# Single-bank accumulators for two Strassen-Winograd products, and three moved pieces around them

## The chip, the cores and the metric

One core of a Trainium2 chip runs the whole program. The metric is the device time of one execution in microseconds. TensorE (PE) multiplies and writes into PSUM, which has eight banks of 512 float32 values in each of 128 partitions. VectorE (DVE) and ScalarE (ACT) read PSUM and write SBUF, GpSimd (POOL) works in SBUF, and SyncE (SP) issues most of the DMAs; POOL issues the stores of the result, which scatter rows.

## The reference, cut to what matters

```python
scores = scale * np.matmul(q, k.transpose(0, 1, 3, 2)) - np.log(S)
x = np.matmul(1.0 / (1.0 + np.exp(-scores)), v)          # 4 x 12 heads, 448 x 64
x = x.transpose(0, 2, 1, 3).reshape(1792, 768)
out[mask] = gate_w[mask, None] * (np.maximum(x[mask] @ w1[e], 0.0) @ w2[e])   # 8 experts, top 1
g = out @ w_gate                                          # 768 -> 1536
h = g * (1.0 / (1.0 + np.exp(-g))) * (out @ w_val)
return h @ w_out                                          # 1536 -> 768
```

The change touches only the last two lines: the gate and value products with the SwiGLU behind them, and the output product.

## The kernel before, in words

Attention and the experts take the first half of the span. From about 500 us on the kernel computes the two last products, each by the seven products of the Strassen-Winograd scheme, n = 1 to 7. Every operand is split into a high part and a residual, and each product is three matmuls (high-high, high-low, low-high).

**First product** (`strassen`, L950): 24 block rows r, each with n = 1..7. Rows 0 to 11 are done on the first half of the tokens, rows 12 to 23 on the second. Even r are gate weights, odd r value weights, so a pair (r, r+1) makes one block of h. One product (r, n) is nine matmuls. The order of the products is the list `steps`. In the pairs (0, 1), (10, 11) and (12, 13) it alternates the two rows for each n, in the order 1, 6, 5, 7, 2, 4, 3 (for the pair (0, 1) both rows of n = 1 and of n = 2 come first); in all other pairs one row is done before the other, in the order 1, 6, 5, 7, 2, 3, 4.

**Accumulators.** n = 1 and then 2 accumulate in a bank called a (tile `pa`), n = 5 and 3 in c (`pc`), n = 7 and 4 in d (`pd`); n = 6 has b (`pb`), from the pool `ps_t` of two banks that the transposes use as well. The tiles a, c and d are made for a pair of rows: one tile of two banks, one bank for each row. `ps_b` holds one such pair tile for a, `ps_a` two for c and d. Waits are kept by tile, so an instruction on one row's bank can have to wait for an instruction on the other row's.

**What empties them** (`evac`): ACT copies n = 1 (L991; the first at L1422) and n = 5 (L997) to SBUF; VectorE adds that copy to n = 6 (L994, u) and n = 7 (L1000, c); after n = 3 and 4 it adds u (L1008); a sigmoid on ACT (L973) and products on VectorE or POOL (L974, L978) finish a tile, and h goes to DRAM (L980, L982).

**Weights** are loaded (`w<-wgd`, L791), some summed by POOL (`sr`, L805), cast by ACT (`wgh`, L828), and VectorE takes the residual (`wgl`, L831), which is issued five products ahead of the matmuls; the sums are kept in DRAM (`wsd`, L835). SP issues loads and stores in the order in which the program emits them. The inputs are transposed by PE (L889) and split by ACT and VectorE (L923, L924). Between the products of this stage blocks of w_out are still prepared for the second product: `room` is loaded (L151), split and combined (L158 to L174, L1310) and stored.

**Second product** (`product2`, L1543): pairs of token blocks q = 0 to 6 with n = 1..7; one product is 18 matmuls. q = 0 and 1 alternate for each n, the others do not. The operand h is cast by ACT (`hhi`, L1500) and its residual taken by VectorE (`hlo`, L1504). The output weights of n = 5, 7, 2, 4, 3 (`wo`, three pieces each) are loaded when the first product ends and split during the first twelve steps (`split_wo`, casts on ACT at L80, residuals on VectorE at L81). The results are evacuated at L1580 to L1599 and stored by POOL: whole rows with `perm_c` (L1561), and for the last block half rows with `permh` (L1566).

Of the kernel before, what the change touches and what calls it, by code (L numbers as in the profile page):

```python
# [9 lines left out]
F32 = mybir.dt.float32  # L10
# [12 lines left out]
def sigmoid_attention_moe_swiglu_kernel(  # L23
# [18 lines left out]
    P = 128  # L42
# [9 lines left out]
    HW = DM // 2  # L52
# [12 lines left out]
    PS = bass.MemoryType.PSUM  # L65
# [113 lines left out]
    with ExitStack() as actx:  # L179
# [7 lines left out]
        ps_t = actx.enter_context(tc.tile_pool(name="ps_t", bufs=4, space=PS))  # L187
# [6 lines left out]
        n = B * G  # L194
# [553 lines left out]
    ectx = ExitStack()  # L748
    early = ectx.enter_context(tc.tile_pool(name="early", bufs=2, side="right", reuse_waits="tile"))
    ps_t = ctx.enter_context(tc.tile_pool(name="pst", bufs=2, space=PS, reuse_waits="tile"))  # L750
    ps_a = ctx.enter_context(tc.tile_pool(name="psa", bufs=2, space=PS, reuse_waits="tile"))
    ps_b = ctx.enter_context(tc.tile_pool(name="psb", bufs=1, space=PS, reuse_waits="tile"))
    mctx = ExitStack()
    wh = mctx.enter_context(tc.tile_pool(name="wh", bufs=LA + 1, reuse_waits="tile"))
    xp = mctx.enter_context(tc.tile_pool(name="xp", bufs=2, reuse_waits="tile"))
# [4 lines left out]
    TH = NT // 4  # L760
# [6 lines left out]
    R1 = 2 * NP  # L767
# [103 lines left out]
    tr = {}  # L871
# [54 lines left out]
    def make_xc(pool, n):  # L926
        xc[n] = tuple(pool.tile([P, K3, TH], F32R, tag=f"x{i}{n}", name=f"x{i}{n}", bufs=1)
                      for i in range(2))

    banks = {}  # L930
    sb = {}

    def strassen(r, n):
        if (r // 2, "a") not in banks:
            banks[r // 2, "a"] = ps_b.tile([P, 2, 512], F32, tag="b", name="pa")
        if n == 5 and (r // 2, "c") not in banks:
            banks[r // 2, "c"] = ps_a.tile([P, 2, 512], F32, tag="a", name="pc")
        if n == 7 and (r // 2, "d") not in banks:
            banks[r // 2, "d"] = ps_a.tile([P, 2, 512], F32, tag="a", name="pd")
        if n == 6:  # L940
            banks[r, "b"] = ps_t.tile([P, 512], F32, tag="tr", name="pb")
            ps = banks[r, "b"][:, :TH]
        else:
            ps = bank(r, {1: "a", 2: "a", 5: "c", 3: "c", 7: "d", 4: "d"}[n])
        hi, lo = wst.pop((r, n))
        xh, xl = xc[n]
        for j in range(K3):
            a = slice(j * P, (j + 1) * P)
            for st, mv, m in ((hi, xh, 0), (hi, xl, 1), (lo, xh, 2)):
                nc.tensor.matmul(ps, st[:, a], mv[:, j],  # L950
                                 start=(j == 0 and m == 0 and n not in (2, 3, 4)),
                                 stop=(j == K3 - 1 and m == 2), skip_group_check=True)

    def bank(r, nm):
        return banks[r // 2, nm][:, r % 2, :TH]

    def et(tag, bufs):
        return evp.tile([P, TH], F32, tag=tag, name=tag, bufs=bufs)
# [26 lines left out]
    def evac(r, n):  # L985
# [19 lines left out]
        else:  # L1005
# [1 line left out]
            t = et("c", 3) if steps[min(k // 14 * 14 + 13, len(steps) - 1)][1] == n else ps  # L1007
            V.tensor_add(t, ps, sb[r, "u"])  # L1008
            finish_tile(k + 1, r, *{3: (1, 2), 4: (2, 1)}[n], t, V)

    turn = [2]

    def wide(name):
        turn[0] += 1
        pool, tag = ((ps_a, "a"), (ps_a, "a"), (ps_b, "b"))[(turn[0] - 1) % 3]
        return pool.tile([P, 2, 512], F32, tag=tag, name=name)

    ev = {}
    nv = {}
# [65 lines left out]
    last = {}  # L1085
# [18 lines left out]
    def plain(kind, s, j):  # L1104
        return kind == 1 and s == L and j >= J32
# [187 lines left out]
    JO = 3  # L1293
    room = {}

    def load_o(j, x):
        load_r64(room["ro", x], ("o", j + x * KD))
# [33 lines left out]
    for j in range(JO):  # L1331
        c = 6 * j
# [52 lines left out]
    with tc.manual_schedule():  # L1385
# [24 lines left out]
        for idx, key in enumerate(seq):  # L1410
            if idx + LA < len(seq) and not plain(*seq[idx + LA]):
                split_w(*seq[idx + LA])
            for f in at.get(key, ()):
                f()
            if key == (1, 2, 0):
                nsl = nc.values_load(nslots[0:1, 0:1], min_val=0, max_val=NS,
                                     skip_runtime_bounds_check_because=why)
            product(*key)
        strassen(0, 1)
        yout(L)  # L1420
        ystore_rows(L)
# [4 lines left out]
        def between():  # L1426
            nonlocal evp, post
            with tc.If(nsl > NS0):
                extra()
            mctx.close()  # L1430
            rctx.close()
            post = ctx.enter_context(tc.tile_pool(name="post", bufs=1, reuse_waits="tile"))
            xcb = gctx.enter_context(tc.tile_pool(name="xcb", bufs=1, reuse_waits="tile"))
            for n in (6, 5, 7, 4, 3):
                make_xc(xcb, n)
            evp = gctx.enter_context(tc.tile_pool(name="evp", bufs=1, reuse_waits="tile"))
# [82 lines left out]
        banks2 = {}  # L1519
        sb2 = {}  # L1520

        def bank2(q, nm):
            return banks2[q // 2, nm][:, q % 2, :HW]

        def product2(q, n):
            if (q // 2, "a") not in banks2:
                banks2[q // 2, "a"] = ps_b.tile([P, 2, 512], F32, tag="b", name="oa")
            for m, nm in ((5, "c"), (7, "d")):
                if n == m and (q // 2, nm) not in banks2:
                    banks2[q // 2, nm] = ps_a.tile([P, 2, 512], F32, tag="a", name="o" + nm)  # L1530
            if n == 6:
                banks2[q, "b"] = ps_t.tile([P, 512], F32, tag="tr", name="ob")
                ps = banks2[q, "b"][:, :HW]
            else:
                ps = bank2(q, {1: "a", 2: "a", 5: "c", 3: "c", 7: "d", 4: "d"}[n])
            wh_, wl_ = wo[n]
            for h in range(2):
                hi, lo = hst.pop((q, n, h))
                for j in range(K3):
                    a = slice(j * P, (j + 1) * P)  # L1540
                    ws_ = slice((h * K3 + j) * HW, (h * K3 + j + 1) * HW)
                    for st, mv, m in ((hi, wh_, 0), (hi, wl_, 1), (lo, wh_, 2)):
                        nc.tensor.matmul(  # L1543
                            ps, st[:, a], mv[:, ws_],
                            start=(h == 0 and j == 0 and m == 0 and n not in (2, 3, 4)),
                            stop=(h == 1 and j == K3 - 1 and m == 2), skip_group_check=True)
# [24 lines left out]
        def later2(i, f):  # L1571
            due2.setdefault(max(i, state2["now"]), []).append(f)

        def evac2(q, n):
            V = nc.vector
            k = place2[q, n] + 1
            last = q == NQ - 1
            if n == 1:
                t = sb2[q, "p1"] = small("p")
                nc.scalar.copy(t, bank2(q, "a"))  # L1580
            elif n == 6:
                t = sb2[q, "u"] = small("u")
                V.tensor_add(t, banks2.pop((q, "b"))[:, :HW], sb2.pop((q, "p1")))
            elif n == 5:
                t = sb2[q, "p5"] = small("p")
                nc.scalar.copy(t, bank2(q, "c"))
            elif n == 7:
                t = out_tile(q, 2)[:, 1]
                V.tensor_add(t, bank2(q, "d"), sb2.pop((q, "p5")))
                V.tensor_add(t, t, sb2[q, "u"])  # L1590
                if last:
                    later2(k, lambda: store(q, 2, 1))
            elif n == 2:
                nc.scalar.copy(out_tile(q, 1)[:, 0], bank2(q, "a"))
                if last:
                    later2(k, lambda: store(q, 1, 0))
            else:
                i, m = {3: (1, 1), 4: (2, 0)}[n]
                V.tensor_add(sb2[q, i][:, m], bank2(q, {3: "c", 4: "d"}[n]), sb2[q, "u"])  # L1599
                later2(k, lambda: store(q, i, m if last else None))  # L1600

        todo = {}

# [34 lines left out]

        for j in range(JO, KD):
            if j <= JO + 1:  # L1640
                key = ((1, 6), (R1 + 1, 5))[j - JO]
                at_step(*key, lambda j=j: next_room(j))
            b0 = ((2, 1), (R1 + 2, 6), (R1 + 2, 6))[j - JO]
            d = 20 * (j == KD - 1)
            for x in range(2):
                for g in range(4):
                    at_step(*b0, lambda j=j, x=x, g=g: convert_o(j, x, g), d + 8 * x + 2 * g)
            for h in range(2):
                at_step(*b0, lambda h=h: combine_o(h), d + 15 + 2 * h)
                at_step(*b0, lambda j=j, h=h: store_o(j, h), d + 17 + h)  # L1650
            if j == JO + 1:
                at_step(*b0, lambda j=j: load_o(j + 1, 0), d + 6)
                at_step(*b0, lambda j=j: load_o(j + 1, 1), d + 14)
# [89 lines left out]
        for i, (q, n) in enumerate(steps2):  # L1743
            product2(q, n)
            later2(i + 1, lambda q=q, n=n: evac2(q, n))
            state2["now"] = i
            while i in due2:
                for f in due2.pop(i):
                    f()
            prep2_to(2 * i + 6)  # L1750
            if i < 10:
                for k in ((3 * i) // 2, (3 * i) // 2 + 1)[:1 + i % 2]:
                    split_wo(*rest[k])
        for i in range(len(steps2), len(steps2) + 3):
            state2["now"] = i
# [63 lines left out]
```

## Time and profile before

| | us |
|---|---|
| median of 3 runs | 1006.51 (1006.0 to 1006.66) |
| profiled execution | 1007.19 |
| its span | 1005.1 |
| PE busy | 970.7 (97%), granted clock 0.994 |
| VectorE busy | 788.7 (78%) |
| ScalarE busy | 586.6 (58%) |
| GpSimd busy | 224.4 (22%) |

PE is busy almost throughout, so the time is PE's work, its few idle places and the tail. A wait is named by the engine that had it and the instruction that ended it. An engine takes its instructions in the order of the program, so a wait holds up all that is queued behind it on that engine.

### The profile page before, as it was taken

How to read it: one execution, taken by the hardware profiler on the slowest of the kernel's cores; microseconds unless marked ns; L12 is line 12 of the kernel's file. 1: busy time of each engine (PE TensorE's matmuls, PEld its weight loads, DVE VectorE, ACT ScalarE, POOL GpSimd, SP SyncE). 2: the span in 40 equal slices, each digit the busy share in tenths (PEclk: the TensorE clock that was granted, in tenths of full speed). 3: DMA queues.
4: the chain of work that ended last, by engine and by line, in shares of the span. 5: the costliest groups of instructions: out<-in, count | busy, mean ns of one | idle time of the engine just before them, and what ended most of it. 6: DMA issues, size and time to landing. Idle time of an engine off the chain costs nothing. (4 is left out here: it accounts for less than half of the span.)

```text
span 1005.1 us, 16210 instructions
## 1 busy us (share of the span) xinstructions
PE 970.7 (97%) x5384; PEld 788.9 (78%) x5384; DVE 788.7 (78%) x1278; ACT 586.6 (58%) x920; POOL 224.4 (22%) x231
## 2 busy tenths in 40 slices
PE   8999999999999999999988999999999999999995
PEld 4555555777767777777877899988999998999995
DVE  7888887978778788766787979888888788866561
ACT  6988883677767777777753544464544544533331
POOL 1000011201132112110136555442122221010101
PEclk9999999999999999999999999999999999999998
DMA  9889879268788857877737475546464768533300
GB/s 339 313 311 348 326 279 362 82 246 308 268 308 296 301 205 211 338 263 280 206 120 242 151 234 163 153 153 219 162 225 153 267 194 296 133 122 115 110 33 31
DMA packets 102521, 222.77 MB, mean 222 GB/s; under 512 B 11760, under 2 KB 59120, under 8 KB 102432
## 3 DMA queue, kind: packets, MB, share of 16 engines
q1 hardware_dynamic: 93872, 188.99, 55.7%
q0 software_dynamic: 6864, 31.68, 8.4%
q10 hardware_dynamic: 1696, 1.02, 0.3%
q8 instruction: 44, 0.72, 0.3%
q14 instruction: 45, 0.37, 0.1%
HBM read 217.89 MB, written 55.66 MB: 272 GB/s over the span
## 5 line engine op out<-in xcount | busy, mean ns | idle before, releaser
L1095 DVE TENSOR_TENSOR wlo<-wraw,whi 128x768 fp32r<-128x768 f32 (+1 forms) x182 | 195.0, 1094 | 64.1 <-ACT whi L1093 60.1
L1093 ACT CAST whi<-wraw 128x768 fp32r<-128x768 f32 (+1 forms) x182 | 166.9, 929 | 84.3 <-PE hps L1142 43.5
L950 PE MATMUL pd<-x,wgh 128*128 128x448 f32 x288 | 83.6, 372 | 4.9 <-DVE h L978 2.5
L950 PE MATMUL pa<-x,wgh 128*128 128x448 f32 x288 | 83.0, 370 | 2.6 <-ACT x L923 2.0
L950 PE MATMUL pc<-x,wgh 128*128 128x448 f32 x288 | 82.9, 369 | 0.3 <-DVE m L974 0.3
L245 ACT ACTIVATE a<-sc,logs 128x896 f32<-128x896 f32 x72 | 68.7, 1005 | 9.5 <-PE sc L253 8.4
L828 ACT CAST wgh<-sr 128x384 fp32r<-128x384 f32 x96 | 48.8, 513 | 42.0 <-PE pd L950 18.4
L831 DVE TENSOR_TENSOR wgl<-sr,wgh 128x384 fp32r<-128x384 f32 x96 | 70.8, 745 | 2.2 <-ACT wgh L828 2.1
L1001 POOL TENSOR_TENSOR c<-u,c 128x448 f32<-128x448 f32 x24 | 34.8, 1454 | 161.6 <-DVE c L1000 161.6
L950 PEld LDWEIGHTS pd<-x,wgh 128*128 128x128 f32 x288 | 53.7, 189 | 11.1 <-issue 6.3
L950 PEld LDWEIGHTS pa<-x,wgh 128*128 128x128 f32 x288 | 54.2, 190 | 7.9 <-ACT x L923 2.3
L286 PE MATMUL pu<-a,vr 128*64 128x448 f32 x288 | 59.2, 547 | 0.0
L950 PEld LDWEIGHTS pc<-x,wgh 128*128 128x128 f32 x288 | 53.8, 188 | 5.4 <-DVE m L974 0.5
L1142 PE MATMUL yps<-whi,hh 128*128 128x384 f32 x208 | 56.8, 354 | 0.0
L1142 PE MATMUL yps<-wlo,hh 128*128 128x384 f32 x208 | 53.8, 339 | 1.4 <-DVE wlo L1095 1.3
L950 PE MATMUL pd<-x,wgl 128*128 128x448 f32 x144 | 53.3, 370 | 0.0
L1142 PE MATMUL yps<-whi,hl 128*128 128x384 f32 x208 | 53.2, 336 | 0.0
L950 PE MATMUL pc<-x,wgl 128*128 128x448 f32 x144 | 52.9, 367 | 0.0
L950 PE MATMUL pa<-x,wgl 128*128 128x448 f32 x144 | 52.6, 365 | 0.0
L1142 PE MATMUL hps<-whi,xh 128*128 128x512 f32 x156 | 50.6, 405 | 0.0
L1142 PE MATMUL hps<-wlo,xh 128*128 128x512 f32 x156 | 49.0, 395 | 1.1 <-DVE wlo L1095 1.1
L1142 PE MATMUL hps<-whi,xl 128*128 128x512 f32 x156 | 48.3, 391 | 0.0
(323 smaller groups left out, 2341.0 us busy)
## 6 DMA issues: line engine op xcount, KB each, us to landing
wraw<-in_moe_w_dram SPq DMA_DIRECT2D x108, 384.0 KB
wraw<-in_moe_w_dram SPq DMA_DIRECT2D x78, 512.0 KB
ring<-in_moe_w_dram SPq DMA_DIRECT2D x30, 512.0 KB
ring<-in_moe_w_dram SPq DMA_DIRECT2D x40, 384.0 KB
w<-wgd SPq DMA_DIRECT2D x36, 384.0 KB
qkr<-in_qkv_dram SPq DMA_DIRECT2D x23, 448.0 KB
hraw<-hd SPq DMA_DIRECT2D x13, 768.0 KB
r<-in_moe_w_gate_dram SPq DMA_DIRECT2D x12, 768.0 KB
```

Source lines behind the costliest of these rows:

```text
L245: nc.scalar.activation(am[key], sc[:, :, :S], AF.Sigmoid, bias=logs, scale=SCALE)
L286: nc.tensor.matmul(pu[h * D:(h + 1) * D, :S], vt[:, i % 2, c, h], a[:, h], start=False, stop=(c == CK - 1))
L828: nc.scalar.copy(hi, s)
L831: nc.vector.tensor_sub(lo, s, hi.bitcast(F32))
L950: nc.tensor.matmul(ps, st[:, a], mv[:, j], start=(j == 0 and m == 0 and n not in (2, 3, 4)), stop=(j == K3 - 1 and m == 2), skip_group_che ...
L1001: nc.gpsimd.tensor_tensor(t, sb[r, "u"], t, op=ALU.add)
L1093: nc.scalar.copy(hi[:, :w], r)
L1095: nc.vector.tensor_sub(lo[:, :w0], r[:, :w0], hi[:, :w0].bitcast(F32))
L1142: nc.tensor.matmul(ps[:, m, :w], st[:, a], mv[:, m * w:(m + 1) * w], start=(j == 0 and i == 0), stop=(j == m_ - 1 and i == 2))
```

## The change

The four edits, in the order of the diff:

1. The accumulators a, c and d of both products become tiles of one bank. a has a pool of two banks (`ps_d`), c and d share a pool of four (`ps_c`), b stays in `ps_t`. `ps_b` is closed just ahead of the first product (0, 1), and `ps_a` in `between()`, right after (1, 1).
2. The load of `room` (a block of w_out) moves from step (1, 6) to step (1, 7).
3. The splits of the output weights' third group (n = 5, 7, 2, 4, 3) come one step later each.
4. The last token block is stored in three pieces, and not in four: the half row after n = 7, the whole row i = 1 after n = 3, the half row after n = 4.

```diff
-    ps_a = ctx.enter_context(tc.tile_pool(name="psa", bufs=2, space=PS, reuse_waits="tile"))
-    ps_b = ctx.enter_context(tc.tile_pool(name="psb", bufs=1, space=PS, reuse_waits="tile"))
+    actx2 = ExitStack()
+    bctx = ExitStack()
+    ps_a = actx2.enter_context(tc.tile_pool(name="psa", bufs=2, space=PS, side="right",
+                                            reuse_waits="tile"))
+    ps_b = bctx.enter_context(tc.tile_pool(name="psb", bufs=1, space=PS, reuse_waits="tile"))
...
     def strassen(r, n):
-        if (r // 2, "a") not in banks:
-            banks[r // 2, "a"] = ps_b.tile([P, 2, 512], F32, tag="b", name="pa")
-        if n == 5 and (r // 2, "c") not in banks:
-            banks[r // 2, "c"] = ps_a.tile([P, 2, 512], F32, tag="a", name="pc")
-        if n == 7 and (r // 2, "d") not in banks:
-            banks[r // 2, "d"] = ps_a.tile([P, 2, 512], F32, tag="a", name="pd")
...
+        ps = open_bank(banks, r, n, "p")[:, :TH]
...
+    def open_bank(banks, r, n, name):
+        nm = {1: "a", 2: "a", 6: "b", 5: "c", 3: "c", 7: "d", 4: "d"}[n]
+        if n in (1, 5, 6, 7):
+            pool, tag = {"a": (ps_d, "a"), "b": (ps_t, "tr")}.get(nm, (ps_c, "c"))
+            banks[r, nm] = pool.tile([P, 512], F32, tag=tag, name=name + nm)
+        return banks[r, nm]
+
+    def single_banks():
+        nonlocal ps_c
+        actx2.close()
+        ps_c = ctx.enter_context(tc.tile_pool(name="psc", bufs=4, space=PS, side="right",
+                                              reuse_waits="tile"))
+
     def bank(r, nm):
-        return banks[r // 2, nm][:, r % 2, :TH]
+        return banks[r, nm][:, :TH]
...
+        bctx.close()
+        ps_d = ctx.enter_context(tc.tile_pool(name="psd", bufs=2, space=PS, reuse_waits="tile"))
         strassen(0, 1)
...
             rctx.close()
+            single_banks()
...
         def product2(q, n):
...
+            ps = open_bank(banks2, q, n, "o")[:, :HW]
...
                 nc.scalar.copy(out_tile(q, 1)[:, 0], bank2(q, "a"))
-                if last:
-                    later2(k, lambda: store(q, 1, 0))
...
-                later2(k, lambda: store(q, i, m if last else None))
+                later2(k, lambda: store(q, i, m if last and n == 4 else None))
...
-                key = ((1, 6), (R1 + 1, 5))[j - JO]
+                key = ((1, 7), (R1 + 1, 5))[j - JO]
...
-            if i < 10:
-                for k in ((3 * i) // 2, (3 * i) // 2 + 1)[:1 + i % 2]:
+            if 1 <= i < 11:
+                k0 = 3 * (i - 1) // 2
+                for k in (k0, k0 + 1)[:2 - i % 2]:
                     split_wo(*rest[k])
```

PE's instructions keep their order; what changes on PE is what they wait for. On the other engines three places change.

SP, at the start of the first product (`w` are the weight loads, `wsd` the stores of sums, `hd` a store of h, `room` the moved load), before:

```order
L791 DMA w<-wgd 128x768
L835 DMA wsd<-sr 128x384
L982 DMA hd<-h 128x448
L151 DMA room<-in_moe_w_out_dram 128x1536 x2
L835 DMA wsd<-sr 128x384
L791 DMA w<-wgd 128x768 x3
L835 DMA wsd<-sr 128x384 x5
```

and in the changed kernel, where the lines have other numbers:

```order
L795 DMA w<-wgd 128x768
L839 DMA wsd<-sr 128x384
L989 DMA hd<-h 128x448
L839 DMA wsd<-sr 128x384
L795 DMA w<-wgd 128x768 x3
L839 DMA wsd<-sr 128x384
L151 DMA room<-in_moe_w_out_dram 128x1536 x2
L839 DMA wsd<-sr 128x384 x4
```

The two room loads move behind three weight loads and two stores.

ACT, at the start of the second product (`wo` are the casts of the output weights, `p` the copies of n = 1), before:

```order
L1500 CAST hhi<-ss 128x384
L80 CAST wo_10103<-wo_10104 128x768
L1580 COPY p<-oa 128x384
L1500 CAST hhi<-s2v 128x384 x2
L80 CAST wo_10103<-wo_10104 128x768 x2
L1580 COPY p<-oa 128x384
L1500 CAST hhi<-ss 128x384 x2
```

and in the changed kernel:

```order
L1503 CAST hhi<-ss 128x384
L1574 COPY p<-oa 128x384
L1503 CAST hhi<-s2v 128x384 x2
L80 CAST wo_10147<-wo_10148 128x768
L1574 COPY p<-oa 128x384
L1503 CAST hhi<-ss 128x384 x2
L80 CAST wo_10147<-wo_10148 128x768 x2
```

Each cast of `wo` moves behind one copy and two casts of h; VectorE's residuals move likewise behind `hlo`.

POOL, the last stores of the result, before:

```order
L1561 DMA out_dram<-ot,perm_c 1792x768 x12
L1566 DMA out_dram<-ot,permh 3584x384 x4
```

and in the changed kernel:

```order
L1555 DMA out_dram<-ot,perm_c 1792x768 x12
L1560 DMA out_dram<-ot,permh 3584x384
L1555 DMA out_dram<-ot,perm_c 1792x768
L1560 DMA out_dram<-ot,permh 3584x384
```

One whole row block takes the place of two half ones.

## Rows read from the trace of the kernel before

**Rows 1.** Waits of PE from 505 us: total, times, longest in us.

```profile
PE pd L950 <- DVE h L978: 2.5, 1, 2.5
PE pd L950 <- DVE c L1000: 2.4, 3, 0.8
PE pa L950 <- ACT x L923: 2.0, 1, 2.0
PE ob L1543 <- DVE hlo L1504: 1.7, 1, 1.7
PE pb L950 <- DVE wgl L831: 1.0, 1, 1.0
PE pa L950 <- ACT p L1422: 0.6, 1, 0.6
PE pc L950 <- DVE m L974: 0.3, 1, 0.3
PE oa L1543 <- DVE hlo L1504: 0.3, 1, 0.3
```

**Rows 2.** Windows: busy us of PE, PEld, DVE, ACT, POOL, granted clock, DMA share, GB/s.

```profile
549.00:552.00 3.00, 3.00 (x10) 2.64 (x9) 2.74 (x6) 0.51 (x1) 0.12 (x1) 0.51 0.73 217
```

**Rows 3.** Windows, behind the wait of 1.7 us in the second product.

```profile
845.40:848.40 3.00, 2.92 (x16) 2.92 (x17) 2.97 (x6) 3.00 (x6) 0.00 (x0) 1.00 1.03 410
```

**Rows 4.** Windows again, the stretch in which VectorE is nearly full.

```profile
529.60:563.60 34.00, 29.54 (x135) 25.70 (x134) 28.06 (x39) 13.27 (x26) 23.23 (x19) 0.95 0.57 188
```

**Rows 5.** Timeline of VectorE there: start, us, instruction, [idle before <-releaser].

```profile
529.07 0.54 DVE L831 TENSOR_TENSOR wgl<-sr,wgh 128x384 fp32r<-128x384 f32 x1
530.65 0.62 DVE L1000 TENSOR_TENSOR c<-pd,p 128x448 f32<-128x448 f32 x1 [1.05 <-PE pd L950]
...
541.20 1.49 DVE L831 TENSOR_TENSOR wgl<-sr,wgh 128x384 fp32r<-128x384 f32 x1
...
562.99 0.61 DVE L994 TENSOR_TENSOR u<-pb,p 128x448 f32<-128x448 f32 x1
```

**Rows 6.** Timeline of PE where it next needs a bank that VectorE empties.

```profile
563.65 0.60 PE L889 MATMUL pt<-ident,yt 112*128 112x112 f32 x4
```

**Rows 7.** Timeline of POOL, the first sum of weights after 524 us.

```profile
532.69 1.00 POOL L805 TENSOR_TENSOR sr<-w 128x384 f32<-128x384 f32 x1 [9.64 <-DMA w<-wgd]
```

**Rows 8.** DMA issues from 515 to 575 us: times, KB each.

```profile
room<-in_moe_w_out_dram SPq DMA_DIRECT2D x2, 768.0 KB
```

**Rows 9.** Timeline of SP: start, us, engine, line, DMA, count.

```profile
524.93 4.60 SPq L791 DMA_DIRECT2D w<-wgd  x3
```

**Rows 10.** Windows, columns as in rows 2: while the room loads are transferred.

```profile
526.00:528.00 2.00, 2.00 (x12) 1.82 (x11) 2.00 (x5) 1.04 (x3) 0.00 (x0) 1.00 1.02 422
```

**Rows 11.** Windows: the middle pairs, and where the second half's inputs are split.

```profile
584.00:657.00 73.00, 73.00 (x371) 66.97 (x370) 59.02 (x89) 29.69 (x61) 41.59 (x37) 1.00 0.55 170
657.00:692.00 35.00, 33.29 (x162) 29.82 (x161) 33.72 (x56) 22.22 (x49) 8.42 (x7) 1.00 0.42 132
```

**Rows 12.** Timeline of ACT, the first cast of the third weights.

```profile
843.13 0.84 ACT L80 CAST wo<-wo 128x768 fp32r<-128x768 f32 x1 [7.32 <-DMA wo<-wod]
```

**Rows 13.** Timeline of VectorE at the same place.

```profile
844.00 0.96 DVE L81 TENSOR_TENSOR wo<-wo,wo 128x768 fp32r<-128x768 f32 x1 [2.10 <-ACT wo L80]
```

**Rows 14.** Chain that ended last: start, us, what; one product.

```profile
886.14 3.18 PE ob L1543 x18
```

**Rows 15.** Timeline of POOL, two whole-row stores.

```profile
969.87 1.00 POOL L1561 DMA_INDIRECT out_dram<-ot,perm_c  x1 [16.58 <-DVE hlo L1504]
973.69 1.29 POOL L1561 DMA_INDIRECT out_dram<-ot,perm_c  x1 [2.83 <-DVE hlo L1504]
```

**Rows 16.** Line L1561, these stores: from issue to landing.

```profile
DMA to landing us min/median/max: 3.0/3.4/4.2
```

**Rows 17.** Timeline of POOL, the last store.

```profile
995.86 0.96 POOL L1566 DMA_INDIRECT out_dram<-ot,permh  x1 [2.36 <-DMA out_dram<-ot,permh]
```

**Rows 18.** Timeline of VectorE, the last result.

```profile
993.88 0.56 DVE L1599 TENSOR_TENSOR ot<-od,u 128x384 f32<-128x384 f32 x1 [2.61 <-PE od L1543]
```

More of the change, by code (lines that the diff above doesn't have):

```diff
@@ L750, in sigmoid_attention_moe_swiglu_kernel @@
     ps_t = ctx.enter_context(tc.tile_pool(name="pst", bufs=2, space=PS, reuse_waits="tile"))
-    ps_a = ctx.enter_context(tc.tile_pool(name="psa", bufs=2, space=PS, reuse_waits="tile"))
-    ps_b = ctx.enter_context(tc.tile_pool(name="psb", bufs=1, space=PS, reuse_waits="tile"))
+    actx2 = ExitStack()
[3 more added lines that the diff above has]
+    ps_b = bctx.enter_context(tc.tile_pool(name="psb", bufs=1, space=PS, reuse_waits="tile"))
+    ps_c = ps_d = None
     mctx = ExitStack()
@@ L933, in strassen @@
     def strassen(r, n):
-        if (r // 2, "a") not in banks:
-            banks[r // 2, "a"] = ps_b.tile([P, 2, 512], F32, tag="b", name="pa")
-        if n == 5 and (r // 2, "c") not in banks:
-            banks[r // 2, "c"] = ps_a.tile([P, 2, 512], F32, tag="a", name="pc")
-        if n == 7 and (r // 2, "d") not in banks:
-            banks[r // 2, "d"] = ps_a.tile([P, 2, 512], F32, tag="a", name="pd")
[L940 to L944, printed above, removed]
+        ps = open_bank(banks, r, n, "p")[:, :TH]
         hi, lo = wst.pop((r, n))
@@ L1009, in evac @@
             finish_tile(k + 1, r, *{3: (1, 2), 4: (2, 1)}[n], t, V)
[L1011 to L1016, printed above, removed]
     ev = {}
@@ L1522, in bank2 @@
         def bank2(q, nm):
-            return banks2[q // 2, nm][:, q % 2, :HW]
+            return banks2[q, nm][:, :HW]
         def product2(q, n):
[L1526 to L1535, printed above, removed]
+            ps = open_bank(banks2, q, n, "o")[:, :HW]
             wh_, wl_ = wo[n]
```

## The prediction

> **What bounds the kernel now.** I read the shares first: PE is busy for 970.7 of 1005.1 us, so only its waits, a fall of its clock and the tail can be gained. Then PE's waits in the half that the change touches [rows 1]: 11.0 us, with one more wait of 0.3 on `hlo` that isn't shown. The reader is to sort them by what ends them. Those on an evacuation (h, c, m, p: 2.5 + 2.4 + 0.6 + 0.3 = 5.8) are waits for a bank. Those on `hlo` (1.7 and twice 0.3) are waits for an operand of the second product. Those on x (2.0) and `wgl` (1.0) are for operands of the first, and no edit touches what makes these. Third, the clock behind the longest wait [rows 2]. Last VectorE in the same stretch, since it ends nearly all of these waits and is itself busy for 28.06 of 34.00 us [rows 4]. On that the forecast turns: PE's waits say what could go, VectorE's idle time says how much of it can.
>
> **Edit 1, the banks of the first product.** With tiles for two rows PE waits for the other row's evacuation, and an evacuation for the other row's product. With single banks each waits for its own alone, and with four banks for c and d a pair no longer waits for the former one. What goes up to 563 us:
> - The bank waits [rows 1]: 0.6 ahead of (1, 1), 0.8 each ahead of (0, 4) and (1, 4), 2.5 ahead of (2, 7), 0.3 ahead of (3, 5), together 5.0. The third wait on c stands at (10, 11), below.
> - The clock. Behind the wait of 2.5 the granted clock is 0.51 from 549 to 552 us [rows 2], the lower level of 1.2 GHz. 3.00 us at 0.51 are 1.5 us of work, so 1.5 go with the wait. Behind the wait of 1.7 it stays at 1.00 [rows 3].
>
> PE alone could thus be 5.0 + 1.5 = 6.5 us ahead at 563 us. But at 563.65 it starts a transpose into a bank of `ps_t` [rows 6] that VectorE's u empties at 562.99 + 0.61 = 563.60 [rows 5], 0.05 us sooner. b stays in `ps_t`, so here PE can lead by no more than VectorE does. VectorE's idle time from 529.60 to 563.60 is 34.00 - 28.06 = 5.9 [rows 4], nearly all of it on PE's products, such as the 1.05 ahead of c [rows 5]. I walked its order with the trace's durations and the new waits. Behind the residual of 529.07 comes c of (0, 7), which no longer waits for (1, 7). About 0.5 of idle time stays at (1, 4), 0.1 at (0, 3), and 0.5 in small hand-overs: 5.9 - 1.1 = 4.8 us of lead at u.
>
> **Edit 2, the room load.** POOL's first sum waited 9.64 us for its weights [rows 7], which stood behind two room loads of 768 KB [rows 8]. At 422 GB/s [rows 10] these take 1.57 MB / 422 GB/s = 3.7 us. Without them in front the sums start about 529.0, and behind them come the casts and residuals that need them; that is why POOL doesn't hold the 4.8 back. The price: the room loads go behind three weight loads, which SP is done with at 529.5 [rows 9], and two stores. Behind two weight loads and the room loads' own 3.7 us they land about 536, and VectorE first wants them about 539 by the walk: 3 us spare. Four stores of sums and one of h follow on SP and wait for POOL or VectorE anyway. So I cost the move at nothing; with the cover gone, a us of lateness would be a us of VectorE's chain. But POOL's sums now lie beside earlier work of VectorE. The residual of 541.20, beside POOL, took 1.49, that of 529.07 only 0.54 [rows 5]. That slowing moves with POOL; I take it as the same sum at another place, and for what it may add I round 4.8 to **4.5**.
> Bounds: above 6.5, PE's own. Below: PE comes to the transpose 2.0 us before u is there (6.5 - 4.5), between the wait of 1.7, behind which the clock held, and that of 2.5, behind which it fell; with a fall, 4.5 - 1.5 = 3.0.
>
> From 584 to 657 us PE has no idle time and VectorE is busy for 59.02 of 73.00 [rows 11]: it has room to follow, and PE keeps its lead. At (10, 11) the third wait on c, 0.7 to 0.8, goes too. But from 657 to 692 VectorE is busy for 33.72 of 35.00, and PE idles 1.71 there [rows 11]; the 1.0 of it on `wgl` comes after the wait on c. What PE gains at (10, 11) it waits longer for `wgl`: **0** (at most 0.8).
>
> **Edit 1 in the second product, with edit 3, the casts.** The first cast of the third weights holds ACT for 7.32 us on a transfer [rows 12], with p and two `hhi` queued behind; VectorE waits 2.10 for that cast [rows 13] with `hlo` behind it, and PE waits 1.7 for `hlo`. One step later p, `hhi` and two `hlo` come first, and need no transfer. I walked ACT and VectorE from there to 880 us: the tightest `hlo` is done 1.1 us before PE wants it, the tightest residual of a weight 2 us. So 1.7 + 0.3 + 0.3 go, **2.2** by their unrounded values. Bounds: 2.3, and half of it, 1.1, if one `hlo` is later than the walk says.
>
> **Edit 4, the stores.** The last result is ready at 993.88 + 0.56 = 994.44 [rows 18] and its store starts at 995.86 [rows 17], since it waits for the store before it. Whole-row stores followed 3.82 apart [rows 15], that is the shortest landing of 3.0 [rows 16] and 0.8. In the changed kernel the store before is a whole row. What it needs is ready one product sooner, 994.44 - 3.18 [rows 14] = 991.26, so it starts about 991.5 and the last one 3.82 later, 995.3, or with landings of 3.4 and 4.2 [rows 16] at 995.7 and 996.5. That is 0.5, 0.1 or -0.6; I take **0.3**, between the first two.
>
> **Sum.** 4.5 + 0 + 2.2 + 0.3 = 7.0 us. 1007.19 - 7.0 = 1000.2 for an execution like the profiled one, which was 0.7 above the median of 1006.51: **999.5**.
>
> The GPSIMD Engine Reference of the Trainium skill (section Key points) says that GpSimd shares its SBUF interfaces with VectorE and contends with VectorE's instructions that have two SBUF inputs, which a residual is. The trace agrees (1.49 against 0.54 [rows 5]); it speaks against pulling POOL's sums into a stretch where PE waits for VectorE. The first rival is what that would do here.
>
> **The rivals.**
> - *VectorE keeps its times.* POOL's sums, 3.7 us earlier, lie beside five residuals that VectorE does between 528 and 535 us, and each goes from 0.54 to 1.49: 5 x 0.95 = 4.7, and the lead of 4.8 is gone. Left are 2.2 + 0.3, so 1004.0. For it: the row of 541.20. Against: the residuals that POOL slowed before are then free of it. 0.15.
> - *All of it.* VectorE does better than the walk, and PE keeps 6.5 + 0.8 + 2.3 + 0.6 = 10.2: 996.3. 0.12.
> - *It doesn't do what it says.* h, c and m are all made by VectorE in one order, so behind each wait removed PE might wait as long for the next one. Then about 1006.5. Against: VectorE's idle time, which the waits for the other row's products make. 0.06.
> - *Slower: the casts come too late.* Five weights are now split one step nearer to their use; PE wants the second of three pieces about a third into a product of 3.18 us [rows 14]. If VectorE is over 2 us later than in my walk, that spare is used up, and each weight costs PE a wait of the size that VectorE had, 2.10 [rows 13]: 5 x 2.1 = 10.5, against 7.0 gained, so 1010.0. For it: VectorE is the engine that is late there today. Against: the transfer on which ACT waited has landed by then. 0.06.
>
> **How the numbers follow.** The forecast has 0.61. Its own bounds give gains from 3.0 + 1.1 - 0.6 = 3.5 to 10.2, 1003.0 to 996.3. The range takes in the first two rivals, **996.0 to 1004.0**, and leaves out the last two and some tail. A measurement of this kernel can tell about 0.2%, 2.0 us, from no change. Faster than that, under 1004.5: 0.61 + 0.12 + most of 0.15 = 0.84. Within it: 0.06 and the rest of the first rival, 0.10. Slower: 0.06.
>
> **What would show it.** In the changed profile PE's waits on h, c and p from 505 to 563 us are gone, the granted clock stays at 1.00 from 540 to 558, POOL's first sum starts near 529, and a new wait on u, at the transposes, of about 2 us stands a little before 560. Without that wait the second rival holds; with one much longer, or slow residuals before 535, the first. The wait on `wgl` near 680 is longer than 1.0. No wait on `hlo` over 0.2 is left, and none on `wo`; waits on `wo` at the heads of products would make the last rival right.

## The result, and the profile after

The changed kernel takes 997.88 us (median of 6, 996.11 to 998.41) against 1006.59 for the kernel before on the same chip; the ratio is 0.991, interval 0.9894 to 0.9925. Forecast were 999.5 in a range of 996.0 to 1004.0. The profiled execution takes 998.37, its span is 996.7. By the profiled executions that is 8.8 us less than before. 0.4 of it arose ahead of the first product and another 0.4 outside the span (1007.19 - 1005.1 = 2.1 against 998.37 - 996.7 = 1.7); no run explains these two.

PE has 5384 matmuls and the same order in both kernels, so each can be set beside its twin. The difference of their starts is PE's lead. It is 0.37 us at the first matmul of the first product, where the changed waits come only later, and 8.31 at the last matmul:

| at | start before | start after | lead | what came since |
|---|---|---|---|---|
| first matmul of (0, 1) | 508.70 | 508.33 | 0.37 | |
| (0, 2) | 515.65 | 512.58 | 3.07 | waits of 0.6 and 2.0 gone |
| (0, 4) | 531.42 | 530.02 | 1.41 | new waits, see below |
| (2, 7) | 548.11 | 543.00 | 5.11 | waits of 0.8 and 2.5 gone |
| (2, 3) | 553.41 | 546.67 | 6.74 | the fall of the clock gone |
| (3, 7) | 564.02 | 559.34 | 4.69 | wait of 0.3 gone, new wait of 2.5 |
| first matmul of the second product | 835.26 | 829.41 | 5.85 | (10, 11) |
| last matmul | 993.51 | 985.20 | 8.31 | hlo |

The waits of PE in the two products of the changed kernel, in the columns of [rows 1] (total, times, longest):

```profile
PE pt L893 <- DVE u L1001: 2.5, 1, 2.5
PE pd L944 <- DVE c L1007: 1.6, 1, 1.6
PE pb L944 <- DVE wgl L835: 0.7, 1, 0.7
PE pd L944 <- DVE wgl L835: 0.6, 1, 0.6
PE ob L1537 <- DVE hlo L1507: 0.5, 1, 0.5
```

The waits for the other row's h, m and p are gone. What is left waits for VectorE. New is u ahead of the transposes, which the forecast had as "about 2 us, a little before 560". Grown is c ahead of (0, 4), from 0.8 to 1.6, and new are 0.6 on `wgl` in (0, 7) and 0.5 on `hlo` in the first product of n = 6; the forecast had none of these three. Where they stand, on PE's timeline:

```profile
524.85 0.47 PE L944 MATMUL pd<-x,wgl 128*128 128x448 f32 x1 [0.58 <-DVE wgl L835]
530.02 0.65 PE L944 MATMUL pd<-x,wgh 128*128 128x448 f32 x2 [1.62 <-DVE c L1007]
...
558.96 0.60 PE L893 MATMUL pt<-ident,yt 112*128 112x112 f32 x4 [2.54 <-DVE u L1001]
```

VectorE's window from the same residual to the same u as in [rows 4] (busy us of PE, PEld, DVE, ACT, POOL, granted clock, DMA share, GB/s), then the windows behind the place of the old wait and behind the new one, as in [rows 2]:

```profile
529.20:558.90 29.70, 26.41 (x130) 23.92 (x130) 28.00 (x39) 13.21 (x26) 24.50 (x19) 1.00 0.79 256
...
549.00:552.00 3.00, 3.00 (x17) 2.77 (x16) 3.00 (x6) 1.88 (x4) 1.01 (x1) 1.00 0.62 229
559.00:562.00 3.00, 3.00 (x19) 2.78 (x20) 2.27 (x4) 1.53 (x4) 0.00 (x0) 1.00 0.54 115
```

That is the argument of the forecast in one row: VectorE does the same work, 28.00 against 28.06 us, in 29.7 instead of 34.0 us. Of its 5.9 us of idle time 1.7 are left. PE gained what VectorE's window got shorter by, 4.3, and not the 6.5 of its own waits and the clock.

POOL's first sum, which waited 9.64 in [rows 7], and the last stores with the input of the whole-row one, in the columns of [rows 15, 17, 18]:

```profile
528.54 1.66 POOL L809 TENSOR_TENSOR sr<-w 128x384 f32<-128x384 f32 x1 [5.76 <-DVE wgl L835]
```

```profile
983.73 0.96 POOL L1555 DMA_INDIRECT out_dram<-ot,perm_c  x1 [5.20 <-DVE ot L1591]
987.51 0.96 POOL L1560 DMA_INDIRECT out_dram<-ot,permh  x1 [2.82 <-DMA out_dram<-ot,perm_c]
...
982.40 0.56 DVE L1591 TENSOR_TENSOR ot<-oc,u 128x384 f32<-128x384 f32 x1 [3.76 <-PE oc L1537]
```

### The profile page after: what moved, and what is told of

It reads as the page before. It is cut to its first block, busy times and chain, and to the rows that moved or that the text cites. A ratio compares the mean times of both kernels' runs of the same rounds, so it can differ in the third digit from the quotient of the medians.

```text
span 996.7 us, 16173 instructions
## 1 busy us (share of the span) xinstructions
PE 967.4 (97%) x5384; PEld 787.4 (79%) x5384; DVE 790.8 (79%) x1278; ACT 589.1 (59%) x920; POOL 222.0 (22%) x230
## 5 line engine op out<-in xcount | busy, mean ns | idle before, releaser
L245 ACT ACTIVATE a<-sc,logs 128x896 f32<-128x896 f32 x72 | 68.8, 1006 | 9.3 <-PE sc L253 8.5
## 6 DMA issues: line engine op xcount, KB each, us to landing
wraw<-in_moe_w_dram SPq DMA_DIRECT2D x78, 512.0 KB
ring<-in_moe_w_dram SPq DMA_DIRECT2D x30, 512.0 KB
```

What stands on the lines that cost most here:

```text
L245: nc.scalar.activation(am[key], sc[:, :, :S], AF.Sigmoid, bias=logs, scale=SCALE)
```

## The experiments

Whole executions of one kernel differ by several us (997.1 to 1002.4 in six of the changed kernel on one chip), but in the profiles most of that lies ahead of the first matmul of (0, 1), which starts anywhere from 506.7 to 511.4 us. So every run is judged by its **stretch**, from the start of that matmul to the start of the last one, and by its **tail**, from the end of the last matmul to the end of the span. The changed kernel was profiled twice, with stretches of 476.87 and 476.64; another kernel twice, with 473.74 and 473.67. So the stretch repeats to 0.3 us in these two kernels. Every other kernel has one profile, and where the clock falls or PE waits behind a transfer it can differ by more: the kernel before and the one with only the room load moved have the same second product, but it took 158.24 and 159.09.

| kernel | stretch | first product | second | tail | ratio to before (interval) |
|---|---|---|---|---|---|
| before | 484.81 | 326.57 | 158.24 | 11.26 | 1 |
| changed | 476.87 | 321.08 | 155.79 | 11.14 | 0.991 (0.9894 to 0.9925) |
| changed, again | 476.64 | 320.94 | 155.70 | 11.13 | 0.9929 (0.9905 to 0.9952) |
| room load back | 481.67 | 326.08 | 155.59 | 11.13 | 0.9955 (0.9937 to 0.9973) |
| casts back | 478.15 | 320.68 | 157.47 | 11.14 | 0.9943 (0.9924 to 0.9962) |
| stores back | 476.72 | 321.08 | 155.64 | 11.25 | 0.9929 (0.9904 to 0.9955) |
| pair tiles back | 479.25 | 323.37 | 155.88 | 11.12 | 0.9939 (0.992 to 0.9959) |
| pair tile for a alone back | 476.25 | 321.13 | 155.12 | 11.13 | 0.9949 (0.9929 to 0.997) |
| before, with the room load moved | 483.12 | 324.03 | 159.09 | 11.27 | 0.9976 (0.9958 to 0.9994) |
| changed, room work later | 473.74 | 318.06 | 155.68 | 11.13 | 0.989 (0.9865 to 0.9915) |

**The yardstick.** The changed kernel beside the experiments on their chip.

> The changed kernel itself, as the yardstick of this chip. Every theory expects 8 to 9 us under the kernel before, about 997.9 us.

1000.04 us against 1006.65, a little less gain than in the first comparison. Its profiled execution took 1001.21 against 998.37, and it starts the stretch at 511.40 instead of 508.33; the stretch itself is no longer.

**The room load back.**

```diff
-                key = ((1, 7), (R1 + 1, 5))[j - JO]
+                key = ((1, 6), (R1 + 1, 5))[j - JO]
```

> The changed kernel with the room load back at step (1, 6). My theory: VectorE sets the lead that PE keeps past the transposes (4.3 us in the changed kernel), and POOL's sums feed it; with the sums 3 to 4 us later again (first one about 532) u comes 1.5 to 3 us later, so the kernel is 1.5 to 3 us slower than the changed one, 999.4 to 1000.9. Rival: single banks are all that counts, VectorE has the slack, within 0.5 us of the changed kernel.

1002.28 us, 2.2 more than the yardstick; the stretch of the profiled execution is 4.8 to 5.0 longer than in the changed kernel, more than any theory had. POOL's first sum, PE's waits and the window behind the wait on u:

```profile
532.86 1.02 POOL L809 TENSOR_TENSOR sr<-w 128x384 f32<-128x384 f32 x1 [9.77 <-DMA w<-wgd]
```

```profile
PE pt L893 <- DVE u L1001: 3.0, 1, 3.0
PE pd L944 <- DVE c L1007: 2.9, 2, 1.6
...
562.00:565.00 3.00, 3.00 (x10) 2.70 (x9) 1.11 (x2) 1.38 (x3) 0.00 (x0) 0.50 0.77 223
```

The sums are late as in the kernel before, a second wait on c comes, u is later, and with the longer wait on u the clock falls to 0.50, the lower level. Of the 5.0, 1.7 are lost up to (3, 5), which PE reaches 47.69 us into the stretch and not 46.01. The longer wait costs 0.5, and the remaining 2.8 are lost where the clock is low. The medians differ by only 2.2, which is what is left without the fall; whether the other executions had it is not known. In this profile, with single banks but the old room load, the first product has only 0.5 of its 5.5 us.

**The casts back.**

```diff
-            if 1 <= i < 11:
-                k0 = 3 * (i - 1) // 2
-                for k in (k0, k0 + 1)[:2 - i % 2]:
+            if i < 10:
+                for k in ((3 * i) // 2, (3 * i) // 2 + 1)[:1 + i % 2]:
```

> The changed kernel with the splits of the third weights where they were. My theory: the waits on hlo are made by ACT's wait for a transfer, whatever the banks, so 1.7 + 0.3 + 0.3 us come back: 2.0 to 2.5 us slower than the changed kernel, about 1000.1. Rival: single banks let ACT and VectorE empty a product sooner, and that alone removed the waits: within 0.5 us of the changed kernel.

1001.45 us; the second product takes 157.47 against 155.79, 1.7 more. ACT, then PE at the old place:

```profile
836.40 0.83 ACT L80 CAST wo<-wo 128x768 fp32r<-128x768 f32 x1 [7.65 <-DMA wo<-wod]
...
838.75 0.44 PE L1537 MATMUL ob<-wo,hlo 128*128 128x384 f32 x1 [1.62 <-DVE hlo L1507]
```

Both theories held in part. The wait of ACT on the transfer and PE's 1.6 behind it come back. The two later waits of 0.3 don't; they stand in both profiles with pair tiles and the old casts, so single banks remove them. In the pair-tile run below the casts take the second product from 158.24 (or 159.09) to 155.88 without single banks, so with the casts moved the banks add next to nothing here (155.70 to 155.79).

**Banks back, the rest kept**, and **the room load alone**: the kernel before with edits 2 to 4, and with edit 2 only, both with the tiles for two rows.

> The kernel before with edits 2, 3 and 4, but the accumulators in tiles for two rows. In the stretch from the first matmul of the first product to the last of the second (484.8 us in the profile before, 476.8 in the changed one), theory A (banks and room load need each other: with late sums VectorE is the bound, with pair tiles PE waits for the other row) expects the waits on h and c to be mostly there again and 480.5 to 482.5 us. Theory B (the room load carries nearly all) expects 478 or less. Theory C (single banks carry nearly all but the casts) expects 483 or more.

> The kernel before with edit 2 alone. In the same stretch (484.8 us before) theory A expects 482 to 484.3: POOL's sums start about 529, but PE's waits for the other row's c and h stay, some shorter. Theory B (the room load carries nearly all) expects 481 or less, without a fall of the clock near 550.

1000.26 and 1004.3 us. The first is between theories A and B, the second where A put it. PE's waits in the second run:

```profile
PE ob L1543 <- DVE hlo L1504: 2.6, 1, 2.6
PE pd L950 <- DVE c L1000: 2.4, 3, 0.8
...
PE pd L950 <- DVE h L978: 0.9, 1, 0.9
```

The three waits on c are those of [rows 1] to the tenth, but the long wait on h has shrunk from 2.5 to 0.9, without a bank touched, and no fall of the clock follows it. So that wait was made of two things: the pair tile, which put PE behind an h that it didn't need, and VectorE, which came late to that h when the room load stood earlier. The first product as a table of two edits:

| first product, us | room load as before | room load moved |
|---|---|---|
| pair tiles | 326.57 | 324.03 |
| single banks | 326.08 | 321.08 |

Alone the room load gives 2.5 and the banks 0.5; together they give 5.5. But both profiles in the left column hold a fall of the clock, and those in the right column none. The falls cost 1.6 (the growth of the lead from (2, 7) to (2, 3)) and 2.8. Without them an estimate is 0.9 for the room load alone, 1.7 for the banks alone and 3.9 together, so the two edits still need each other, but less. Past (3, 7) the picture is simpler: single banks for c and d give 1.0 us in the pair (10, 11), 25.75 against 26.73, and 0.2 behind it, in every run that has them. From (3, 7) to the second product it is 269.8 to 270.2 us with them and 271.2 without; with the room load back it is 272.6, since the slow clock lies there.

**a as a pair again.**

```diff
+            if nm == "a":
+                if r % 2 == 0:
+                    pair = pool.tile([P, 2, 512], F32, tag=tag, name=name + nm)
+                    banks[r, nm], banks[r + 1, nm] = pair[:, 0], pair[:, 1]
...
-        ps_d = ctx.enter_context(tc.tile_pool(name="psd", bufs=2, space=PS, reuse_waits="tile"))
+        ps_d = ctx.enter_context(tc.tile_pool(name="psd", bufs=1, space=PS, reuse_waits="tile"))
```

> The changed kernel with the accumulator of n = 1 and 2 as one tile for two rows again, c and d as single banks. The wait of 0.6 on p ahead of (1, 1) comes back, and PE reaches the branch between the experts and this stage later, so the wait of 2.0 that also went comes back too: PE is 2.5 us later at (0, 2). My theory: VectorE holds PE at (0, 4) and at the transposes in either kernel, so the stretch (476.8 us in the changed kernel) is 476.8 to 477.6. Rival: PE's own waits set the time, 479.3.

The stretch is 476.25, not longer at all, and its first product takes 321.13 as in the changed kernel; why the second is 0.6 shorter was not tried. The whole time, 1001.73, is longer than the changed kernel's 997.88 and 1000.04. The profiled execution took 998.49; the three longest of the five have a mean clock of 0.992 or 0.993 against its 0.996, and where they lost their time is not known. PE's waits (u's line is 1006 here, five lines being added ahead of it):

```profile
PE pt L893 <- DVE u L1006: 1.8, 1, 1.8
PE pa L944 <- ACT x L927: 1.6, 1, 1.6
...
PE pa L944 <- ACT p L1429: 0.6, 1, 0.6
```

PE reaches (0, 2) 6.58 us into the stretch and not 4.25, and (0, 4) at 21.68 and not 21.69. The two waits that the change removes at the start of the stage are worth nothing as long as VectorE holds PE at (0, 4).

**Four stores again.**

```diff
                 nc.scalar.copy(out_tile(q, 1)[:, 0], bank2(q, "a"))
+                if last:
+                    later2(k, lambda: store(q, 1, 0))
...
-                later2(k, lambda: store(q, i, m if last and n == 4 else None))
+                later2(k, lambda: store(q, i, m if last else None))
```

> The changed kernel with the four half-row stores of the kernel before at the end. From the end of the last matmul to the end of the span the profiles have 11.3 us before and 11.2 in the changed kernel. My theory: the last store starts 1.4 us behind its input with four stores, and 1.3 with three, so 0 to 0.3 us slower at the tail. Rival: one store less on POOL saves its 1 us: 0.8 to 1.2 slower.

The tail is 11.25 against 11.13 or 11.14: 0.1 us. It is 11.26 in the kernel before and 11.27 in it with the room load moved, which have four stores, and 11.12 to 11.14 in all others.

**VectorE's room work later.** If the new wait on u is VectorE's own load, taking load away ahead of it must remove it. In the walked stretch VectorE does five pieces of room work, 5.1 us, and ACT two, 1.8 us.

```diff
-            b0 = ((2, 1), (R1 + 2, 6), (R1 + 2, 6))[j - JO]
+            b0 = ((3, 5), (R1 + 2, 6), (R1 + 2, 6))[j - JO]
```

> The changed kernel with VectorE's and ACT's work on room begun at (3, 5) instead of (2, 1), behind the u on which PE waits. My theory: the new wait of 2.5 us ahead of the transposes is VectorE being late by its own load; 4 to 5 us of room work out of the way, u is there in time, PE's lead past the transposes is 6.5 to 7 us instead of 4.3, and the kernel is 1.5 to 2.5 us faster than the changed one, 995.4 to 996.4. Rival: VectorE is full later as well (the splits of the second half of the inputs), so the same wait stands on wgl near 680 us and the time stays within 0.5 us of the changed kernel.

995.81 us, and a stretch of 473.74: 3.0 less, more than the 1.5 to 2.5 that I expected. The wait on u is gone:

```profile
PE pd L944 <- DVE c L1007: 1.6, 1, 1.6
PE pb L944 <- DVE wgl L835: 0.6, 1, 0.6
```

The wait on `wgl` near 680 does not grow, so the rival falls. The edit takes ACT's room work out as well, but ACT is busy for only 13.2 of the 29.7 us in the window above and VectorE for 28.0. This kernel is better than both; a second series gave

> The changed kernel with the room work begun at (3, 5), a second time, as the yardstick for the kernel that also moves residuals to POOL: all theories expect a stretch of 473.5 to 474.0 us and about 995.5 us.

995.67 us, a ratio of 0.9912 (0.9883 to 0.9941), and 473.67.

**The room load back, with the room work later.** This one was to show why the room load costs 5 us.

> The changed kernel with the room load back at step (1, 6), but the work on room begun at (3, 5). It parts two ways in which the early room load can cost 4.9 us of the stretch. If it is by the sums, late because their weights stand behind it (my theory), the sums start about 532 again and hold VectorE although the room work is out of its way: 476 to 478.5 us. If it is VectorE's amount of work alone, the stretch is within 1 us of 473.7.

```profile
535.25 1.01 POOL L809 TENSOR_TENSOR sr<-w 128x384 f32<-128x384 f32 x1 [10.47 <-DMA w<-wgd]
...
PE pt L893 <- DVE u L1001: 0.4, 1, 0.4
```

One execution was taken, 997.78 us. Its stretch is 474.26, 0.5 longer. My theory falls: the sums are as late as ever (24.9 us into the stretch, against 20.2 in the changed kernel), and it hardly matters. Late sums by themselves hardly hold PE. In these runs they cost more only with the room work ahead of the u that PE waits for: then VectorE can't catch up.

**Residuals given to POOL.** The waits left are VectorE's at (0, 4), so three of its residuals there went to POOL, ahead of a stretch in which POOL is idle.

```diff
-            at_step(*key, lambda n=n: split_all(0, n))
+            at_step(*key, lambda n=n: [split_x(0, n, j, nc.gpsimd if n == 4 else None) for j in range(K3)])
```

> The changed kernel with the room work begun at (3, 5), and besides the three residuals of the input of n = 4 in the first token half taken by POOL and not by VectorE, at a place where POOL is idle (about 523 to 527 us). In it the waits left in the first product are 1.6 on c ahead of (0, 4) and 0.6 on wgl, both made by VectorE, which is without idle time there. My theory (VectorE's load ahead of (0, 4) is what holds PE): both go, and the stretch from the first matmul of the first product to the last of the second is 471.5 to 472.5 us against 473.7 without the move. Rival (POOL beside VectorE slows VectorE as much as it takes off): 473.3 or more.

996.5 us, a stretch of 474.25 against 473.7: the rival holds. (Of the 0.5, the first product has 0.2; the rest is in the second.) POOL with the three residuals and its next sum, and VectorE beside it:

```profile
520.68 4.05 POOL L928 TENSOR_TENSOR x<-rx,x 128x448 fp32r<-128x448 f32 x3
524.68 1.40 POOL L809 TENSOR_TENSOR sr<-w,sr 128x384 f32<-128x384 f32 x1
...
521.01 1.25 DVE L835 TENSOR_TENSOR wgl<-sr,wgh 128x384 fp32r<-128x384 f32 x1
522.19 0.61 DVE L1001 TENSOR_TENSOR u<-pb,p 128x448 f32<-128x448 f32 x1
522.72 0.99 DVE L835 TENSOR_TENSOR wgl<-sr,wgh 128x384 fp32r<-128x384 f32 x1
...
524.17 2.94 DVE L928 TENSOR_TENSOR x<-rx,x 128x448 fp32r<-128x448 f32 x3
```

and the same three groups of VectorE, behind the residuals that it then still had, in the kernel without the move:

```profile
520.27 2.35 DVE L928 TENSOR_TENSOR x<-rx,x 128x448 fp32r<-128x448 f32 x3
522.55 0.54 DVE L835 TENSOR_TENSOR wgl<-sr,wgh 128x384 fp32r<-128x384 f32 x1
...
523.55 0.54 DVE L835 TENSOR_TENSOR wgl<-sr,wgh 128x384 fp32r<-128x384 f32 x1
...
524.55 1.69 DVE L928 TENSOR_TENSOR x<-rx,x 128x448 fp32r<-128x448 f32 x3
```

2.35 us are taken off, and 0.71 + 0.45 + 1.25 = 2.41 come on; the last of the three lies mostly beside POOL's sum, which the residuals had pushed back. The GPSIMD Engine Reference of the Trainium skill (section Key points) says that GpSimd shares its SBUF interfaces with VectorE and contends with VectorE's instructions that have two SBUF inputs. The trace agrees: here the contention costs the whole of what was moved, and u, which reads PSUM, keeps its 0.61 beside POOL.

## Why the prediction was right

The mechanism was right, and the sum came within 1.1 us (7.0 forecast, 8.1 from the first matmul of the stage on in the two profiles; 8.7 by the first medians, 6.6 by those of the yardstick). Term by term:

- **VectorE as the limit up to 563 us.** Forecast 4.5, from a walk that gave 4.8; measured 55.33 - 51.01 = 4.3 at (3, 7), counted from the start of the stretch. PE's wait on u is 2.5 where "about 2" stood. The walk left 1.1 of idle time; 1.7 stayed, 1.0 of it on PE's products of (0, 4) and (1, 4) (ahead of 532.13 and 533.99) and 0.7 on ACT's cast of a weight (ahead of 535.29). That VectorE is the limit is shown and not only argued: with the room work moved the wait goes and 3.0 are gained, and giving PE back its old waits at the start costs nothing.
- **PE's own waits.** I kept the wait of 2.0 named after x as an operand wait that no edit touches. The name misled: in the changed kernel (0, 2) starts at 512.58, before ACT's cast of that x begins at 513.87, and with pair tiles the same wait is named after a branch of PE's queue in two runs (`PEq L1428`, 2.2 and 1.6; see the last section). It went with the one of 0.6, and two waits came or grew that I had not: 0.6 on `wgl` and 1.6 on c at (0, 4). Since VectorE holds PE there anyway, these errors cancelled; the run with a as a pair shows that both old waits can come back for nothing. The bound of 6.5 was too low for the same reason: PE led by 7.3 at (3, 5), the last product ahead of the transposes, 6.9 of it since the start of the stretch.
- **The clock.** 1.5 forecast, and the lead grew by 6.74 - 5.11 = 1.63 over that place. The clock stays at 1.00 behind the new wait of 2.5 too.
- **The room load.** Cost of nothing: right. The sums begin at 528.5, as said. But I gave it a side role ("that is why POOL doesn't hold the 4.8 back"). Without it the banks bring 0.5 of 5.5 in the profiles, 1.7 of 3.9 without the falls of the clock. And the path is not the one I drew: the run with the room load back and the room work later, a single execution, has the sums as late as before and loses only 0.5. Late sums by themselves hardly hold PE; VectorE's full schedule does.
- **(10, 11).** Forecast 0, measured 1.2. The step that failed is "what PE gains it waits longer for `wgl`": the wait went from 1.0 to 0.7, while PE gained the 0.7 on c. That step took VectorE's work up to that residual as fixed and its start into the split of the inputs as tied to PE. It began 6.3 us earlier where PE led by 4.7. VectorE and ACT there, before and after:

```profile
657.62 2.52 DVE L924 TENSOR_TENSOR x<-rx,x 128x448 fp32r<-128x448 f32 x3 [2.34 <-ACT x L923]
656.59 0.54 ACT L991 COPY p<-pa 128x448 f32<-128x448 f32 x1 [3.33 <-PE pa L950]
```

```profile
651.28 3.70 DVE L928 TENSOR_TENSOR x<-rx,x 128x448 fp32r<-128x448 f32 x3 [0.56 <-ACT x L927]
650.08 0.54 ACT L998 COPY p<-pa 128x448 f32<-128x448 f32 x1 [1.50 <-PE pa L944]
```

  ACT's copy of (10, 1) had to wait until (11, 1) was done too, since both wrote one tile; ACT's casts of x are queued behind that copy, and VectorE behind these. Single banks end that, but it isn't what shortened the wait. With a as a pair again VectorE starts late once more, at 4.87 us after (10, 1) as before and not at 3.22:

```profile
653.33 2.58 DVE L928 TENSOR_TENSOR x<-rx,x 128x448 fp32r<-128x448 f32 x3 [2.22 <-ACT x L927]
```

  Yet the wait on `wgl` is 0.7 there and the pair takes 25.75 us as in the changed kernel. What differs as well is VectorE's busy time from (10, 1) to the end of that wait: 30.66 us before, 31.77 changed, 29.11 with a as a pair, for the same 50 instructions. So VectorE's time there isn't a fixed amount, and why the residual came early enough stays open.
- **The casts.** Forecast 2.2, measured 2.45. With pair tiles the casts give 2.4 or more; with single banks they give 1.7 to 1.8, since these remove the two waits of 0.3 by themselves. The forecast gave the two edits one term, which fits. A wait of 0.5 came on `hlo` at the first product of n = 6, where the kernel before had none and the forecast allowed 0.2.
- **The stores.** Forecast 0.3, measured 0.1. The whole-row store starts 0.8 and not 0.2 after its input (983.73 against 982.40 + 0.56), and the last one 3.78 later, as in [rows 15].
- **The rivals.** The first, VectorE slowed by POOL's earlier sums, did not come: VectorE's work in the window is 28.00 against 28.06. Its mechanism is real, as the run with residuals on POOL shows at full price, but here the sum stayed the same. The late casts didn't come; no wait on `wo` is in the list.

## What to carry to other kernels

When one engine waits for another, add up the idle time of the engine that is waited for before adding up the waits: as long as its work stays the same, that is the most that can be gained. Here it gave 4.8 by the walk and 4.3 as measured, where the waits and the clock gave 6.5. Two small edits can each look weak alone and still be worth taking together (0.5 and 2.5 gave 5.5 in the profiles), because each leaves the other's wait in place; look first whether a fall of the clock sits in one of the profiles, as it does here. The name on a wait is inferred: the wait of 2.0 bore the name of an operand and was a branch. Work that nobody waits for yet, such as the room work here, belongs behind the instruction on which the bounding engine waits; moving it gave 3.0 us for the change of one step.

## What the runs showed of the hardware

- The granted clock fell to its lower level, 0.5, with a wait of PE of 2.51 us (before) and of 3.01 us (room load back), and stayed at 1.00 behind waits of 2.54 (changed), 2.58 (`hlo`, room load alone) and 2.59 (c, residuals on POOL). I had expected the length of the wait to decide it; these rows say that it doesn't alone.
- A wait of 0.6 us cost PE 2.7. Behind (1, 1) stands a branch, which PE's queue works on while the matmuls ahead of it run. The branch in the kernel before and in the changed one (count, duration in ns, start):

```profile
L1428 PEldq COMPARE_BRANCH  x1: 3832/3832/3832, 511.7 to 511.7; - x1
```

```profile
L1430 PEldq COMPARE_BRANCH  x1: 3362/3362/3362, 508.6 to 508.6; - x1
```

  It takes 3.4 to 3.8 us in either, but starts 3 us sooner where (1, 1) doesn't wait. In the changed kernel it ends at 512.0, ahead of the last matmul of (1, 1) at 512.4; before, it ends at 515.5, and PE has been idle since 513.7. The same branch takes 0.05 to 0.07 us on the other engines.
- POOL's scattered stores wait for the landing of the one before and start 0.8 us behind it: 3.8 us apart for whole rows with the shortest landing of 3.0 [rows 15, 16], 3.3 to 3.4 for half rows with landings of 2.6 (before).
